# An FFT-mixing and gated feed-forward kernel on one core: batch 0 is turned on the TensorE instead of through DRAM

## The chip, the cores and the metric

The kernel runs on one core of a Trainium2 chip. The metric is the device time of one execution in microseconds (us). A number called "the time" is a median over several executions. Every kernel here was timed in alternation with the kernel before on the same chip. A program on one core has no second die to compare with, so an execution counts as fast unless it is over 1.5% above the fastest of its kernel.

Engines are named as in the profile: PE is the TensorE's matmuls, PEld its weight loads (loads of the stationary operand), DVE the VectorE, ACT the ScalarE, POOL the GpSimd, SP the SyncE, which issues DMAs here. "Granted clock" is the share of full speed that the TensorE's clock gate granted, so 0.50 is half speed.

## The reference

```python
def _attn_ref(x):                       # x: (8, 3008, 256) float32
    X = np.fft.fft(x, axis=1)
    X = np.fft.fft(X, axis=2)
    return X.real.astype(np.float32)

def _moe_ref(x, w_gate, w_val, w_out):  # x: the above as (24064, 256); weights 256x1536, 256x1536, 1536x256
    gate = np.maximum(x @ w_gate, 0.0)
    val = x @ w_val
    return (gate * val @ w_out).astype(np.float32)
```

## The kernel before

Each batch has 3008 = 94 x 32 rows. Row 32a + j of x lies on partition a, and a transform of 94 points over a is done for each of the 32 residues j (stage 1). Its result is `t1`, a tile of 96 partitions. A transform over the 32 residues follows (stage 2), and for it the residues must lie on partitions: `t4`, 128 partitions by 12 groups. The 256-point transform over the columns is folded into the weights (`fold_w`, three blocks of two matrices with a cosine and a sine part, on the PE), because x is folded about its middle column. From then on the kernel is a long pipeline of steps: two gate matmuls, value matmuls, elementwise products on ACT, DVE and POOL, and output matmuls. The first 12 steps have no output matmuls yet. They carry the rest of the weight folds instead.

For all batches but the first, x is loaded and folded ahead of time on POOL. Batch 0 has no such time, so its products use the unfolded rows: four matmuls for each row, with 96-column tables as the stationary operand and x as the moving one.

```python
def first_products(c, upper):                    # batch 0, stage 1; c = 0..7, two rows for each c
    if not upper:
        psf[c] = early("ps1")
    for i in range(2):
        jj = 2 * c + i
        o = psf[c][0:96, i * D:(i + 1) * D]
        v = xt[0]["hi"][...] if upper else xt[0]["lo"][0:NA, jj, :]
        back = free(v, D - 1, [-1, H - 1])       # the row read backwards
        ...                                      # (cut: which table is which)
        for k, (lo, hi, w, rhs) in enumerate(((0, H + 1, ce, v[:, 0:H + 1]), (1, H, ce, back),
                                              (H + 1, D, up, v[:, 1:H]), (H + 1, D, dn, back))):
            nc.tensor.matmul(o[:, lo:hi], lhsT=w, rhs=rhs, start=not (upper or i or k),
                             stop=upper and i == 1 and k == 3, skip_group_check=True)
```

The change of partitions goes through DRAM, for batch 0 as for the others, and one column then needs a rotation:

```python
def shuffle_out(b, c0, c1, q=nc.sync):
    q.dma_start(out=view(Td[b], 2 * c0 * D, [[16 * D, 96], [1, 2 * (c1 - c0) * D]]),
                      in_=t1t[b][:, 2 * c0:2 * c1, :].rearrange("p j d -> p (j d)"))

def shuffle_in(b, a0, a1):
    ...
    nc.sync.dma_start(out=t4t[b][:, a0:a1, :],
                      in_=view(Td[b], a0 * 128 * D, [[D, 128], [128 * D, a1 - a0], [1, D]]))

def rotate(b, a0=0, a1=NKA, evac=nc.scalar.copy):
    t4 = t4t[b]
    ps = borrow("psr") if b or a0 else early("psr")
    nc.tensor.matmul(ps[:, a0:a1], lhsT=rot[:], rhs=t4[:, a0:a1, H], start=True, stop=True)
    evac(t4[:, a0:a1, H], ps[:, a0:a1])
```

The start of the program, in the order in which it is issued, cut to its core:

```python
WARM = 16
def warm(n):                                     # dummy matmuls on zeros, 512 columns each
    for k in range(n):
        nc.tensor.matmul(psk[:], lhsT=wk[:, 512:640], rhs=wk[:, 0:512], start=True, stop=True)
warm(WARM)
...                                              # loads, tables; then, in three groups:
group((1, 2, 3), False); ...; group((1, 2, 3), True); ...; shuffle_out(0, 1, 4)
group((4, 5), False); group((4, 5), True); ...; shuffle_out(0, 4, 6)
group((6, 7, 0), False); group((6, 7, 0), True); ...
shuffle_out(0, 6, 8); shuffle_out(0, 0, 1, nc.scalar)
...
shuffle_in(0, 0, 4); shuffle_in(0, 4, NKA)
...
warm(10)
pair_w(0, 0, dve)                                # sums and differences of weight blocks
...
fold_w(0, 0, 0, "act"); fold_w(0, 0, 1, "dve"); fold_w(0, 1, 0, "act")   # during the shuffle
rotate(0, 0, 4, dve.tensor_copy)
stage2(0, 0, 0, "act"); stage2(0, 0, 1, "dve")
fold_w(0, 1, 1, "act")
```

`group(cs, upper)` calls `first_products(c, upper)` for each c.

The later batches' work is placed at numbered steps. For batch 1 the shuffle is at step 25 and its rotation at step 29, where PE meets the wait:

```python
    sh, tr, t2 = (22, 28, (29, 30, 32, 34, 35, 37)) if b else (25, 29, (30, 31, 33, 34, 35, 37))
    at(t0 + sh, shuffle_out, b + 1, 0, 8)
    at(t0 + sh, shuffle_in, b + 1, 0, NKA)
    at(t0 + tr, rotate, b + 1)
    for i, k in enumerate(t2):
        at(t0 + k, stage2, b + 1, i // 2, i % 2, "act")
```

## Time and profile before

| What | Value | View |
|---|---|---|
| time | 629.67 us (629.32 to 629.78, 3 runs) | timed runs |
| span of the profiled execution | 630.0 us (its device time was 632.18) | page |
| products of batch 0 on PE | 7.42 to 15.1 us | timeline of PE |
| DRAM shuffle of batch 0 | out 3.65 us, in 2.89 us | chain of waits |
| first gate matmul, first output matmul | 24.57 us, 55.70 us | timeline of PE |
| PE's wait on batch 1's shuffle | 2.05 us, up to 92.84 us | timeline of PE |
| PE busy from 200 to 600 us | 398.79 of 400 us | table by stretches |

Two lines of the page of the kernel before: the busy time of each engine with its share of the span and the number of instructions, and the granted clock in tenths for 40 equal slices (about 15.8 us each; 9 means 90% or more).

```profile
PE 614.4 (98%) x4288; PEld 411.3 (65%) x4320; DVE 537.9 (85%) x644; ACT 439.4 (70%) x842; POOL 513.4 (81%) x439
PEclk9899999999999999999999999999999999999999
```

PE is busy nearly always, so a change of the start is worth what it does to PE's start and no more. Next, the timeline of PE in the kernel before: start in us, duration in us, engine, line, operation, output and inputs, stationary rows x columns, moving rows x columns, count; in brackets an idle time before it and what released it.

```profile
7.42 0.33 PE L197 MATMUL ps<-lo,w 94*96 94x129 bf16 x3
7.59 0.22 PE L197 MATMUL ps<-lo,n 94*96 94x127 bf16 x1
7.64 0.33 PE L197 MATMUL ps<-lo,w 94*96 94x129 bf16 x3
...
22.42 0.17 PE L216 MATMUL psr<-t,rot 128*128 128x4 bf16 x1 [1.77 <-DMA t<-Td]
...
24.57 0.59 PE L555 MATMUL G<-pq,wc 128*128 128x496 bf16 x1
...
55.70 0.60 PE L619 MATMUL po<-wo,h 128*128 128x256 bf16 x4
```

Four product matmuls take 0.22 us (7.42 to 7.64): PE streams columns almost without a pause. After the last product PE does dummies and weight folds, and then waits 1.77 us for the shuffle. The chain of waits of the kernel before (start, length, what) has the shuffle in full:

```profile
15.76 3.65 DMA Td<-t
19.49 2.89 DMA t<-Td
```

The waits of PE in the kernel before (what waited, for what: us in total, times, longest):

```profile
PE psr L216 <- DMA t<-Td: 3.8, 2, 2.0
PE V L570 <- DVE h L583: 2.0, 3, 0.9
```

The first line holds both shuffles that PE waits for: 1.77 us for batch 0 and 2.05 us for batch 1. The table by stretches of the kernel before gives, after the stretch and its length in us, the busy us (instructions) of PE, PEld, DVE, ACT and POOL, the granted clock, the DMA share and GB/s:

```profile
6.00:12.00 6.00, 6.00 (x86) 5.15 (x84) 4.48 (x17) 3.88 (x10) 5.69 (x16) 1.00 1.07 188
12.00:18.00 6.00, 5.88 (x64) 4.17 (x65) 5.12 (x17) 3.19 (x9) 1.82 (x7) 1.00 0.86 303
18.00:24.00 6.00, 4.20 (x24) 1.57 (x20) 3.22 (x6) 1.75 (x3) 0.00 (x0) 0.98 0.56 172
24.00:30.00 6.00, 5.38 (x18) 1.75 (x16) 2.80 (x6) 3.39 (x6) 3.71 (x4) 0.74 1.10 393
```

After the idle time near 21 us the clock falls for about 3 us (0.74 on average from 24 to 30 us).

### The profile page before, as it was taken

How to read it: one execution, taken by the hardware profiler on the slowest of the kernel's cores; microseconds unless marked ns; L12 is line 12 of the kernel's file. 1: busy time of each engine (PE TensorE's matmuls, PEld its weight loads, DVE VectorE, ACT ScalarE, POOL GpSimd, SP SyncE). 2: the span in 40 equal slices, each digit the busy share in tenths (PEclk: the TensorE clock that was granted, in tenths of full speed). 3: DMA queues.
4: the chain of work that ended last, by engine and by line, in shares of the span. 5: the costliest groups of instructions: out<-in, count | busy, mean ns of one | idle time of the engine just before them, and what ended most of it. 6: DMA issues, size and time to landing. Idle time of an engine off the chain costs nothing.

```text
span 630.0 us, 11979 instructions
## 1 busy us (share of the span) xinstructions
PE 614.4 (98%) x4288; PEld 411.3 (65%) x4320; DVE 537.9 (85%) x644; ACT 439.4 (70%) x842; POOL 513.4 (81%) x439
## 2 busy tenths in 40 slices
PE   9899989999999999999999999999999999999996
PEld 6225656666666666666666666666666666666665
DVE  7677978998988998998988988899988989899991
ACT  5357768777777777777777777777687777766660
POOL 7358998998989998998989999899988866565664
PEclk9899999999999999999999999999999999999999
DMA  8878146613734254622725146432722123312113
GB/s 180 272 158 160 43 132 180 152 33 89 213 89 105 66 172 104 162 61 64 209 76 147 34 117 191 105 101 50 214 75 71 33 83 99 78 32 66 35 34 98
DMA packets 34737, 69.01 MB, mean 110 GB/s; under 512 B 5963, under 2 KB 23058, under 8 KB 31346
## 3 DMA queue, kind: packets, MB, share of 16 engines
q1 hardware_dynamic: 29974, 52.85, 31.5%
q0 software_dynamic: 4432, 15.11, 9.9%
q8 instruction: 33, 0.54, 0.4%
q10 hardware_dynamic: 272, 0.30, 0.2%
q14 instruction: 26, 0.21, 0.1%
HBM read 39.63 MB, written 30.96 MB: 112 GB/s over the span
## 4 chain that ended last, share of the span: by engine, by line
PE 93%; DMA 3%; POOL 1%; issue 1%; DVE 1%; ACT 0%; POOLq 0%; DVEq 0%; SPq 0%
PE po L619 39%; PE V L570 19%; PE G L555 10%; PE G L562 10%; PE G L556 9%; PE ps L159 2%; PE ps L228 2%; PE psw L285 1%; DMA Td<-t 1%; DMA t<-Td 1%; DMA lo<-in_x_dram 1%; DVE h L583 1%; PE ps L197 0%; POOL hi L129 0%; PE ps L163 0%
## 5 line engine op out<-in xcount | busy, mean ns | idle before, releaser
L590 POOL TENSOR_TENSOR h<-gm,E 128x992 bf16<-128x992 f32 (+1 forms) x138 | 319.7, 2317 | 79.1 <-DVE E L597 49.6
L619 PE MATMUL po<-wo,h 128*128 128x256 bf16 (+2 forms) x2304 | 328.5, 272 | 0.5
L619 PEld LDWEIGHTS <-h 128*128 128x128 bf16 (+2 forms) x2304 | 231.4, 103 | 105.9
L564 ACT ACTIVATE gm<-G 128x496 f32<-128x496 f32 (+1 forms) x288 | 170.4, 592 | 94.5 <-PE G L562 85.0
L583 DVE TENSOR_TENSOR h<-gs,V 128x1024 bf16<-128x1024 f32 (+3 forms) x150 | 173.8, 1159 | 63.1 <-PE V L570 43.2
L577 DVE SCALAR_TENSOR_TENSOR E<-nb,af,V 128x496 f32<-128x496 bf16 (+1 forms) x276 | 190.1, 730 | 0.0
L557 ACT ACTIVATE gs<-G 128x497 f32<-128x497 f32 (+2 forms) x288 | 169.6, 589 | 25.4 <-PE G L556 25.4
L597 DVE SCALAR_TENSOR_TENSOR E<-E,V 128x992 f32<-128x992 f32 (+1 forms) x138 | 164.4, 1191 | 0.0
L555 PE MATMUL G<-pq,wc 128*128 128x497 bf16 (+2 forms) x288 | 108.4, 376 | 1.2
L562 PE MATMUL G<-pq,wm 128*128 128x496 bf16 (+1 forms) x288 | 108.1, 375 | 0.1
L556 PE MATMUL G<-pq,ws 128*128 128x497 bf16 (+2 forms) x288 | 108.2, 376 | 0.0
L570 PE MATMUL V<-pq,ws 128*128 128x512 bf16 (+2 forms) x279 | 83.7, 375 | 0.0
L570 PE MATMUL V<-pq,wc 128*128 128x496 bf16 (+2 forms) x266 | 80.9, 375 | 0.0
L556 PEld LDWEIGHTS <-ws 128*128 128x128 bf16 x288 | 28.2, 98 | 32.8 <-issue 0.3
L632 ACT COPY os<-po 128x512 f32<-128x512 f32 x63 | 36.9, 585 | 14.7 <-PE po L619 13.0
L570 PEld LDWEIGHTS <-wc 128*128 128x128 bf16 x288 | 28.2, 98 | 21.9 <-issue 3.8
L110 POOL TENSOR_TENSOR eo<-xla 94x254 bf16<-94x254 f32 x56 | 40.1, 727 | 1.1
L555 PEld LDWEIGHTS <-wc 128*128 128x128 bf16 x288 | 28.2, 98 | 19.1 <-issue 1.9
L174 ACT CAST t<-ps 96x512 bf16<-96x512 f32 x60 | 35.0, 583 | 5.6 <-PE ps L197 3.2
L107 POOL TENSOR_TENSOR xla<-xla,xha 94x510 f32<-94x510 f32 x28 | 35.4, 1264 | 2.2
L110 POOL TENSOR_TENSOR eo<-xlb 94x254 bf16<-94x254 f32 (+1 forms) x42 | 34.2, 814 | 0.8
L562 PEld LDWEIGHTS <-wm 128*128 128x128 bf16 x288 | 28.2, 98 | 7.0 <-issue 3.5
(119 smaller groups left out, 360.1 us busy)
## 6 DMA issues: line engine op xcount, KB each, us to landing
out_dram<-os SPq DMA_DIRECT2D x124, 128.0 KB
Td<-t SPq DMA_DIRECT2D x7, 768.0 KB
t<-Td SPq DMA_DIRECT2D x7, 768.0 KB
out_dram<-os SPq DMA_DIRECT2D x82, 64.0 KB
xla<-in_x_dram SPq DMA_DIRECT2D x7, 720.0 KB
xlb<-in_x_dram SPq DMA_DIRECT2D x7, 640.0 KB
nb<-Nd SPq DMA_DIRECT2D x23, 128.0 KB
out_dram<-os SPq DMA_DIRECT2D x40, 48.0 KB
```

The costliest lines, as they stand in the source:

```text
L110: yield eng.tensor_tensor(e1[:, :, o:o + H - 1], x1[:, :, 1:H], free(x1, D - 1, [D, n], [-1, H - 1]), op=op)
L555: nc.tensor.matmul(G[:, ds], lhsT=wc[0][:, fs], rhs=pq[:, 0, ds], start=True, stop=False)
L556: nc.tensor.matmul(G[:, ds], lhsT=ws[0][:, fs], rhs=pq[:, 1, ds], start=False, stop=True)
L557: nc.scalar.activation(pair(t, "gs")[:, t % 2, ds], G[:, ds], ACTF.Relu)
L562: nc.tensor.matmul(G[:, cols], lhsT=wm[0][:, f * 128:(f + 1) * 128], rhs=pqt[b, blk][:, 1, cols], start=False, stop=True, skip_group_check ...
L564: nc.scalar.activation(pair(t, "gm")[:, t % 2, cols], G[:, cols], ACTF.Relu)
L570: nc.tensor.matmul(pair(t, "V")[:, t % 2, cs], lhsT=w[:, f * 128:(f + 1) * 128], rhs=pqt[b, blk][:, min(k, 1), cs], start=(k == 0), stop=( ...
L577: nc.vector.scalar_tensor_tensor(pair(t, "E")[:, t % 2, cols], nbt[b, blk][:, cols], af[:, f:f + 1], pair(t, "V")[:, t % 2, cols], op0=ALU ...
L583: nc.vector.tensor_tensor(pair(t, "h")[:, k, 0, 0:ds.stop - ds.start], pair(t, "gs")[:, k, ds], pair(t, "V")[:, k, ds], op=ALU.mult)
L590: eng.tensor_tensor(free(pair(t, "h")[:], 1024 * (t % 2) + 512 + w - 1, [1024, n], [-1, w]), pair(t, "gm")[:, k, cols], val[:, k, cols], o ...
L597: nc.vector.scalar_tensor_tensor(E[:, :, cols], E[:, :, cols], 2.0, V[:, :, cols], op0=ALU.mult, op1=ALU.subtract)
L619: nc.tensor.matmul(po[0:m, i, :], lhsT=pair(t - f + ff, "h")[:, ff % 2, sg, g * 128:g * 128 + m], rhs=wo[:, ff, :], start=(ff == 0), stop= ...
```

## The change

The intent is to get rid of batch 0's way through DRAM. Stage 1 of batch 0 exchanges its operands: a row of x (128 columns of it) becomes the stationary operand and the tables (192 columns, both halves side by side) the moving one. The result then has the columns of x on its partitions, and matmuls with a permutation matrix ("uprights") can turn it so that the residues lie on partitions for stage 2. The permutation also does what the rotation did.

The half rows that the kernel before read backwards as moving operand become stationary ones, and for them reversed copies (`back`) are made on DVE and ACT beforehand. Column 0 of x has no mirror partner. It is added to lane 0 of the second half by a matmul of its own, whose stationary operand has one column. So each of the 32 rows now has two matmuls with 128 stationary columns and one with one column. The diff, cut to its core:

```diff
-WARM = 16
+WARM = 11
+FIRST = 15
...
+    def first_products(c, upper, k):
+
+        if not (upper or k):
+            psf[c] = early("ps1")
         for i in range(2):
             jj = 2 * c + i
-            o = psf[c][0:96, i * D:(i + 1) * D]
...
-            for k, (lo, hi, w, rhs) in enumerate(((0, H + 1, ce, v[:, 0:H + 1]), (1, H, ce, back),
-                                                  (H + 1, D, up, v[:, 1:H]), (H + 1, D, dn, back))):
-                nc.tensor.matmul(o[:, lo:hi], lhsT=w, rhs=rhs, start=not (upper or i or k),
-                                 stop=upper and i == 1 and k == 3, skip_group_check=True)
+            o = psf[c][:, 192 * i:192 * i + 192]
+            v = xt[0]["hi" if upper else "lo"][0:NA, r % 16, :]
...
+            if k:
+                nc.tensor.matmul(o, lhsT=tabs["back"][:, r, :], rhs=up, start=False, stop=upper and i == 1,
+                                 skip_group_check=True)
+                continue
+            nc.tensor.matmul(o, lhsT=v[:, H:D], rhs=dn, start=not (upper or i), stop=False, skip_group_check=True)
+            nc.tensor.matmul(o[0:1, 96:192], lhsT=v[:, 0:1], rhs=dc, start=False, stop=False, skip_group_check=True)
...
+    def upright(blk, cs, evac):
...
+        for g in range(4):
+            nc.tensor.matmul(ps[:, g * H:(g + 1) * H], lhsT=free(t1t[0][:], 1536 * cs + 128 * (4 * blk + g), [1, 128]),
+                             rhs=perm[:], start=True, stop=True)
...
         def group(cs, upper):
-            for c in cs:
-                first_products(c, upper)
+            for k in range(2):
+                for c in cs:
+                    first_products(c, upper, k)
...
-        shuffle_in(0, 0, 4)
-        shuffle_in(0, 4, NKA)
...
-        warm(10)
...
-        rotate(0, 0, 4, dve.tensor_copy)
+        fold_w(0, 0, 0, g_tile())
+        upright(0, 0, "act")
+        upright(0, 1, "dve")
+        fold_w(0, 0, 1, g_tile())
         stage2(0, 0, 0, "act")
         stage2(0, 0, 1, "dve")
...
-        sh, tr, t2 = (22, 28, (29, 30, 32, 34, 35, 37)) if b else (25, 29, (30, 31, 33, 34, 35, 37))
+        sh, tr, t2 = (22, 28, (29, 30, 32, 34, 35, 37)) if b else (25, 30, (31, 32, 33, 34, 35, 37))
```

Also cut: most sums and differences of weight blocks move from DVE to POOL, one fold moves behind the first gate, four uprights go into steps 1 to 6, batch 1's stage 1 and its rotation are re-spaced, and POOL's folding of the later batches' x and the order of some loads are rearranged.

## The prediction

> **What bounds the kernel.** The busy table gives PE 98% of the 630.0 us span; from 200 to 600 us PE is busy 398.8 of 400. The change leaves that alone. What it can move is the start: in the chain of waits the first gate matmul comes at 24.6 us, the first output matmul about 55 us.
>
> **The start in the trace.** The x loads keep the DMA engines near full to 12.2 us. Products follow to 15.1, then eviction 0.59, DRAM shuffle out 3.65, in 2.89, rotation, two stage-2 evictions, gate at 24.57. PE fills the hole with dummies and weight folds, yet idles from 20.65 to 22.42; the granted clock (table by stretches) then reads 0.50 from 24 to 27 us, about 1.7 us lost. The Trainium skill ("TensorE: Matmul & The Clock Gate", Part 1) describes such half-clock windows of about 3.4 us after an idle one; here a gap of 1.8 us was enough. From 24.6 to 55.0 the twelve steps take 30.4 us; PE is busy 27.6 of them; it waits 2.0 us for DVE h, behind weight pairings on DVE (one took 2.33 us, the others 0.69). At 90.2 PE waits 2.0 us for batch 1's shuffle.
>
> **Removed:** batch 0's shuffle (6.54 us on the chain), its rotation, fifteen dummy matmuls, most pairings on DVE.
>
> **Added:**
> - 32 reversals split between DVE and ACT: ten ops, together about 2 us on each (estimate from 0.58 us for 512 elements on ACT, 0.36 to 0.7 on DVE).
> - Products: 96 matmuls again, no change.
> - Six uprights (4 matmuls, about 0.24 us, and an eviction of 0.58 on ACT or 0.69 on DVE each); two lie before the gate.
> - Pairing moves to POOL, 1.27 us an op, six more ops: 7.6 us. POOL was idle from 14.2 to 26 and 33 to 40, so it fits, narrowly.
> - Longer last products: the reversals of rows 12 to 19 must follow the last loads, and the c=0 product waits in PSUM order for the c=4 eviction, which queues on ACT behind those reversals and two sines. I expect PE to idle about 2 us near 13 to 15 us, products done at about 17.5 instead of 15.1, perhaps a half-clock window after.
>
> **Sum.** Last products 17.5 (+2.4), eviction 0.9, fold 1.1 interleaved, uprights with eviction 1.2, stage 2 with eviction 1.3, gate near 22 (21.5 to 23.8): 1 to 3 us gained. One fold (1.05 us) moves behind the gate and takes part back; a half-clock window avoided is worth up to 1.7. Steps 0 to 11: stalls on DVE h mostly gone, 1 us of PE added: 1 to 2 us gained. Batch 1's rotation comes a step (2 us) later, its stage 1 ends earlier: its 2.0 us wait goes. Total about 5 us.
>
> **Prediction: 624.8 us, 80% range 621.3 to 628.6.** Faster by over 2%: 3%; within 2%: 96%; slower by over 2%: 1%.
>
> **Right if:** no shuffle DMA before 60 us; gate at 21.5 to 23.8; first output matmul at 50 to 53 us; no wait on batch 1's shuffle over 0.5 us; 200 to 600 us unchanged within 0.5 us.
>
> **Wrong if:** PE idle while ACT and DVE do reversals costs half-clock through stage 1 and the folds; weight pairs on POOL arrive late and steps 0 to 6 stall; delayed folds on POOL push batch 1's stage 1, restoring or enlarging the wait at 90 us. A larger gain, if no half-clock window falls.

## More of the kernel before

A sine fold ends with a scaled copy, `wm`, which reads the copy just made and not PSUM:

```python
    plain(ws[i][:, sl_], ps[:])
    nc.vector.tensor_scalar(wm[i][:, sl_], ws[i][:, sl_], scalar1=s2[:], scalar2=None, op0=ALU.mult)
```

## The result, and the profile after

The kernel after takes 636.88 us (636.09 to 637.15, 4 runs) against 629.72 us (629.32 to 630.85, 4 runs) of the kernel before in the same rounds. The ratio is 1.0109, with a 95% interval of 1.0091 to 1.0126. Ratios here are the mean time of one kernel's fast runs over that of the other's of the same rounds, so they are not quite the ratio of the medians quoted. The change costs about 1%. The prediction had a gain of 0.8%, and the result lies outside its range.

The same two lines of the page, for the kernel after:

```profile
PE 623.3 (98%) x4264; PEld 412.4 (65%) x4295; DVE 539.7 (85%) x647; ACT 442.2 (70%) x847; POOL 509.9 (80%) x446
PEclk7599999999999999999999999999999999999999
```

PE is still 98% busy, but it is busy 9 us longer, and the clock is 0.7 and then 0.5 in the first two slices. The timeline of PE in the kernel after, with the columns as above:

```profile
6.46 0.24 PE L215 MATMUL ps<-wn,lo 94*128 94x192 bf16 x1 [0.84 <-DVE wn L429]
6.63 0.26 PE L216 MATMUL ps<-wn,lo 94*1 94x96 bf16 x1
6.83 0.26 PE L215 MATMUL ps<-wn,lo 94*128 94x192 bf16 x1
...
10.00 0.34 PE L215 MATMUL ps<-wn,hi 94*128 94x192 bf16 x1
10.27 0.26 PE L216 MATMUL ps<-wn,hi 94*1 94x96 bf16 x1
10.46 0.34 PE L215 MATMUL ps<-wn,hi 94*128 94x192 bf16 x1
...
31.63 0.38 PE L602 MATMUL G<-pq,wc 128*128 128x496 bf16 x1
...
62.48 0.60 PE L666 MATMUL po<-wo,h 128*128 128x256 bf16 x4
```

The distance from one matmul to the next is what counts here, not the durations, which overlap. A pair of a 128-column and a one-column matmul takes 0.37 us at full clock (6.46 to 6.83; 0.38 over several pairs) and 0.46 us at half clock (10.00 to 10.46). The products end at 26.3 us, so they take 19.8 us instead of 7.7. The weight loads of the kernel after show why a pair is slow. In this timeline of PEld a line without a bracket had no idle time that the profile puts down to anything:

```profile
8.82 0.77 PEld L212 LDWEIGHTS <-back 94*128 94x128 bf16 x6
10.00 0.10 PEld L215 LDWEIGHTS <-hi 94*128 94x128 bf16 x1 [0.41 <-DMA hi<-in_x_dram,ixf]
10.27 0.08 PEld L216 LDWEIGHTS <-hi 94*1 94x1 bf16 x1 [0.17 <-issue]
```

The one-column load starts at 10.27 us, the very time at which its matmul is recorded, and 0.17 us after the load before it had ended. The PE loads, streams, and only then loads again. At full clock the sum agrees: the two loads take 0.10 and 0.08 us, and a pair that needn't wait for its loads takes 0.183 us (the run fullcol, below), in all 0.37 of the 0.38 us measured. In the run of six `back` loads at 8.82 us there is no such gap. The table by stretches of the kernel after:

```profile
6.00:12.00 6.00, 5.50 (x27) 2.63 (x27) 4.29 (x23) 2.98 (x8) 5.59 (x13) 0.69 1.05 179
12.00:18.00 6.00, 6.00 (x30) 2.98 (x29) 4.51 (x11) 2.82 (x8) 5.39 (x13) 0.50 0.56 181
18.00:24.00 6.00, 6.00 (x31) 3.03 (x30) 2.32 (x6) 0.82 (x2) 1.20 (x1) 0.50 0.37 111
```

From 12 to 24 us PE is counted busy all the time, yet the clock is at half, and only 30 matmuls (of 192 or 96 moving columns) go through in 6 us where the kernel before had 64 to 86 (most of about 128). PE's busy time does not show this. The Trainium skill warns of it ("Perfetto Trace Analysis", Identifying the Most-Contended Engine): matmul busy time is a poor measure of how near the PE is to its peak, and the busy share of the weight loads is a better one. This trace agrees: the loads' busy time falls from 5.15 and 4.17 of 6 us before to 2.98 after. Last, the waits of PE in the kernel after:

```profile
PE psk L390 <- DVE wk L384: 1.3, 1, 1.3
PE V L617 <- DVE h L630: 1.1, 2, 0.6
```

The waits on a shuffle are gone. The two profiled spans (630.0 and 635.2 us) therefore add up like this: gate 7.06 us later; first output matmul 6.78 us later; batch 1's wait of 2.05 us gone; PE idle for 0.50 us more from 100 to 200 us (99.29 busy us against 99.79); in sum 6.78 - 2.05 + 0.50 = 5.2 us. From 200 to 600 us PE is busy 398.79 us in both. The profiled execution of the kernel before was a slower one of its kind (632.18 us), which is why the spans differ by less than the medians.

### The profile page after: what moved, and what is told of

It is laid out like the page before. It is cut to its first block, busy times and chain, and to the rows that moved or that the text cites. A ratio compares the mean times of both kernels' runs of the same rounds, so it can differ in the third digit from the quotient of the medians.

```text
span 635.2 us, 11938 instructions
## 1 busy us (share of the span) xinstructions
PE 623.3 (98%) x4264; PEld 412.4 (65%) x4295; DVE 539.7 (85%) x647; ACT 442.2 (70%) x847; POOL 509.9 (80%) x446
## 4 chain that ended last, share of the span: by engine, by line
PE 94%; DVE 2%; DMA 1%; issue 1%; SPq 1%; ACT 0%; POOL 0%; POOLq 0%; DVEq 0%
PE po L666 39%; PE V L617 18%; PE G L602 10%; PE G L609 9%; PE G L603 9%; PE psw L324 2%; PE ps L163 2%; PE ps L266 2%; PE ps L215 1%; PE ps L216 1%; PE ps L212 1%; DMA t<-Td 1%; DMA Td<-t 1%; SPq L717 1%; DVE h L630 0%
## 5 line engine op out<-in xcount | busy, mean ns | idle before, releaser
L114 POOL TENSOR_TENSOR eo<-xla 94x256 bf16<-94x256 f32 (+1 forms) x56 | 35.1, 638 | 0.8
L178 ACT CAST t<-ps 96x512 bf16<-96x512 f32 x56 | 32.7, 584 | 2.4 <-PE ps L163 0.2
L114 POOL TENSOR_TENSOR eo<-xlb 94x256 bf16<-94x256 f32 (+3 forms) x42 | 29.9, 712 | 0.9
```

The source lines that it names most:

```text
L114: yield eng.tensor_tensor(e1[:, :, k * (H + 1):k * (H + 1) + H - k], free(x1, H - k, [D, n], [-1, H - k]), x1[:, :, H + k:D], op=op)
```

## The experiments

Twelve kernels were run. The rival theories for the 12 us that the products lost were:

- A: matmuls with 128 and with one stationary column in turn keep the PE from loading weights ahead, and the sparse stream that follows drops the clock.
- B: the clock falls because of too few dummies or of idle gaps, and the products are slow only because of the clock.
- C: the tables as moving operand, read with a stride, stream slowly.

The first four runs were timed together. In their rounds the kernel before took 631.70 us, 1.5 to 1.9 us more than in the later rounds: four of its seven runs there had a mean clock of 0.994 to 0.996. So "as fast as before" is a mild test in these four.

### no_onecol: the one-column matmuls taken away (wrong result)

```diff
-            nc.tensor.matmul(o[0:1, 96:192], lhsT=v[:, 0:1], rhs=dc, start=False, stop=False, skip_group_check=True)
```

> The 32 one-column matmuls of the products are left out (the result is wrong on purpose: one term of one row is missing). Theory A (changing between a 128-column and a 1-column weight stops weight loads from running ahead, which doubles the product stage and starves the clock gate): the product matmuls start about 0.08 us apart at full clock, the last ends at 15 to 17.5 us, first gate at 21 to 24 us, total 623 to 628 us. Theory B (the shortened warm-up and the gaps while loads arrive let the clock drop, whatever the matmuls are): the clock still reads 0.50 from about 8 us on and the products last beyond 20 us, total above 632 us.

630.19 us against 631.70 of before; ratio 0.9994 (0.9963 to 1.0024). The result was wrong as planned (relative error 0.033). The gate comes at 23.81 us instead of 31.63. So nearly all of the loss goes with 32 small matmuls, although the clock still falls to 0.50 from 10.4 to 20.7 us. A low clock by itself is not the main cost. Two parts of A's expectation missed: the products end at 18.6 us (15 to 17.5 expected), and the total lies above its range. This kernel removes the matmul, its strided moving operand and the change of width together, so it can't tell A from C; the next run does.

### fullcol: the same matmuls with 128 stationary columns (wrong result)

```diff
-            nc.tensor.matmul(o[0:1, 96:192], lhsT=v[:, 0:1], rhs=dc, start=False, stop=False, skip_group_check=True)
+            nc.tensor.matmul(o[:, 96:192], lhsT=v[:, 0:H], rhs=dc, start=False, stop=False, skip_group_check=True)
```

> The one-column matmuls stay, with the same moving operand and its stride, but take 128 columns as weights instead of 1 (wrong on purpose). Theory A: as good as leaving them out plus 32 x 0.04 us, so 624 to 629 us, pairs about 0.13 us apart at full clock. Theory C (the moving operand that hops 1535 elements is what is slow): the pairs stay 0.38 us apart at full clock and 0.47 at half, total 635 us or more. Theory B: 635 us or more.

629.85 us against 631.70; ratio 0.9975 (0.9934 to 1.0015). The relative error is 0.26, as the edit adds columns that don't belong there. The number of matmuls and the moving operand are as in the kernel after; only the loads are larger. The timeline of PE in fullcol:

```profile
6.54 0.26 PE L216 MATMUL ps<-wn,lo 94*128 94x96 bf16 x1
6.64 0.25 PE L215 MATMUL ps<-wn,lo 94*128 94x192 bf16 x1
6.73 0.26 PE L216 MATMUL ps<-wn,lo 94*128 94x96 bf16 x1
```

A pair now takes 0.19 us here (6.54 to 6.73; 0.183 over more of them) instead of 0.38, though it loads 256 columns instead of 129. The larger load is the faster one because all widths are equal. C falls, and so does the idea that the one-column load is itself slow. (With the stationary width the edit also widens the output from one partition to 128; these two can't be parted.) The clock was at 0.50 from 9.6 to 23.2 us here too, after idle gaps of 0.28 and 0.61 us, and still the time was that of before: the order of the widths is the larger share of the loss. The total is just above A's range (624 to 629).

### warm16: the five dummies put back

```diff
-WARM = 11
+WARM = 16
```

> Only the warm-up goes back from 11 to 16 dummy matmuls. Theory A: PE is dense to about 7.6 us instead of 5.6, but the product stage stays sparse and drops the clock all the same: 635 to 638 us, clock 0.50 for at least 12 us in the product stage. Theory B: clock stays at 1.0 for most of the products, total 624 to 630 us.

637.48 us against 631.70; ratio 1.0107 (1.0071 to 1.0142), the same as the kernel after. The clock fell at 11.0 us instead of 8.3 and stayed at 0.50 until 28. The first output matmul came at 63.44 us. A longer warm-up delays the fall and saves nothing: B in its first form falls. Before the clock fell, PE was idle for only 0.15 us (6.31 to 6.46 us) from the first dummy on.

### grouped: the same matmuls, the one-column ones in a pass of their own

```diff
-            if k:
+            if k == 2:
                 nc.tensor.matmul(o, lhsT=tabs["back"][:, r, :], rhs=up, start=False, ...)
                 continue
+            if k == 1:
+                nc.tensor.matmul(o[0:1, 96:192], lhsT=v[:, 0:1], rhs=dc, start=False, ...)
+                continue
             nc.tensor.matmul(o, lhsT=v[:, H:D], rhs=dn, start=not (upper or i), stop=False, ...)
-            nc.tensor.matmul(o[0:1, 96:192], lhsT=v[:, 0:1], rhs=dc, start=False, ...)
...
-            for k in range(2):
+            for k in range(3):
```

> Correct result: within each group all 128-column products come first, then all one-column ones, then the reversed ones, so the width of the weights changes three times a group instead of at every matmul. Theory A, as a matter of changes of width: one-column matmuls run about 0.05 to 0.08 us apart, products end at 16 to 19 us, total 624 to 630 us. Theory A', that a one-column matmul is slow whatever stands before it: they stay 0.15 to 0.2 us apart, total 630 to 635 us. Theory B: no change, 636 to 638 us.

630.34 us against 631.70; ratio 0.9983 (0.9951 to 1.0015), with a right result. Nothing was taken away; only the order of the same matmuls differs from the kernel after. The timeline of PE in grouped:

```profile
6.01 0.66 PE L218 MATMUL ps<-wn,lo 94*128 94x192 bf16 x6
6.59 0.78 PE L216 MATMUL ps<-wn,lo 94*1 94x96 bf16 x6
```

Six one-column matmuls take 0.78 us with the latency of the last one, about 0.10 us from one to the next (A expected 0.05 to 0.08 and a total of at most 630 us, A' 0.15 to 0.2). That is what the same matmul costs with 128 stationary columns in fullcol (0.183 less 0.084 us), so one column isn't slow among its like. The products end at 19.3 us, the gate is at 25.01 and the first output matmul at 56.38. The clock still reads 0.50 from 15.9 to 22.7 us, so grouping cures the order and leaves a second fault, the gaps in PE's work.

### before_onecol: the one-column matmuls added to the kernel before, on zeros

```diff
                 nc.tensor.matmul(o[:, lo:hi], lhsT=w, rhs=rhs, start=not (upper or i or k), ...)
+                if k == 0:
+                    nc.tensor.matmul(o[0:1, 0:96], lhsT=v[:, 0:1], rhs=wk[0:NA, 0:96], start=False, stop=False,
+                                     skip_group_check=True)
```

> The kernel before, plus the suspected cost alone: 32 one-column matmuls put between its 96-column product matmuls, with the same x column as weights and zeros as moving data (adds nothing, the result stays correct). Theory A (changes of weight width serialise and starve the clock): each costs about 0.25 us at full clock, so the product stage grows by 8 us or more, the clock falls to 0.50 within it, and the total rises by 6 to 14 us to 636 to 644 us. Rival (the products were slow in the changed kernel for another reason, such as weights taken from x): rise of at most 32 x 0.04 = 1.3 us.

636.06 us against 630.18; ratio 1.0089 (1.0071 to 1.0108), and the result is right, as `wk` holds zeros. So the loss can be put into the kernel before by this alone. The timeline of PE:

```profile
7.52 0.22 PE L197 MATMUL ps<-lo,w 94*96 94x129 bf16 x1
7.67 0.20 PE L200 MATMUL ps<-wk,lo 94*1 94x96 bf16 x1
7.81 0.31 PE L197 MATMUL ps<-lo,w 94*96 94x127 bf16 x2
...
8.01 0.22 PE L197 MATMUL ps<-lo,w 94*96 94x129 bf16 x1
```

A row takes 0.49 us (7.52 to 8.01) where before it took 0.22, and the products last from 7.52 to 23.3 us, 8.1 us longer than before. Half of the expectation missed: the clock did not fall (0.998 on average). As an estimate from the 0.22 us of a 512-column matmul at full clock, the five matmuls of a row stream 606 columns in 0.26 us, so PE streams about half of the time here, and about a third of it in the kernel after (288 columns, 0.12 of 0.38 us). Half was enough to keep the clock up here; that share alone doesn't decide, for in fullcol a pair streams about two thirds of its time (0.12 of 0.183 us), and after two gaps the clock fell all the same.

### before_tr30: batch 1's rotation a step later, in the kernel before

```diff
-        sh, tr, t2 = (...) if b else (25, 29, (30, 31, 33, 34, 35, 37))
+        sh, tr, t2 = (...) if b else (25, 30, (31, 32, 33, 34, 35, 37))
```

> The kernel before with one part of the change alone: batch 1's rotation at step 30 instead of 29, its first two stage-2 pieces one step later. My reading that PE waited 2.0 us there for the shuffle and that one step (about 2 us) hides it: wait under 0.5 us, total 1.5 to 2.1 us lower, about 0.9970 of before. Rival (the shuffle ends later still or PE only waits elsewhere): within 0.3 us of before.

628.32 us against 630.18 in five rounds; ratio 0.9965 (0.9949 to 0.9980). PE's wait on batch 1's shuffle is gone. This small part of the change is worth having alone, and needs nothing else of it. In the profiled execution part of it went into another wait: PE waited 1.6 us for DVE's E.

### dense: grouped, and nine dummies in the gaps

```diff
+                    if not (upper or k):
+                        warm({0: 4, 5: 1}.get(c, 0))
                     first_products(c, upper, k)
+            if 1 in cs:
+                warm(1 if upper else 3)
```

> The grouped order plus nine dummy matmuls of 512 columns where PE idled in the product stage (three and one after the first group, one before c=5, four before c=0). Theory D (what is left of the loss is the half clock from 16 to 22.6 us, which the idle PE caused): clock stays 1.0, last product at 17 to 18 us instead of 19.3, first gate at 21.5 to 22.5 instead of 25.0, total 2.5 to 3.5 us below grouped, 0.993 to 0.996 of before. Rival (the one-column matmuls count as idle for the gate and it falls all the same): no more than 0.7 us below grouped.

629.03 us against 630.18; ratio 0.9969 (0.9954 to 0.9985). The table by stretches of dense, to be set beside the same stretch of the kernel after:

```profile
12.00:18.00 6.00, 6.00 (x56) 4.11 (x55) 5.61 (x12) 2.26 (x6) 5.12 (x12) 1.00 0.68 219
```

The clock is 1.00 throughout, and the gate comes at 22.74 us, inside the range predicted for the whole change (21.5 to 23.8). The sizes that theory D named for this run were missed: the last product ends at 18.5 us (17 to 18 expected), the gate is 0.24 us late, and the ratio is not in 0.993 to 0.996. The first output matmul is at 55.43, later than predicted: 32.69 us lie between the two, where the kernel before has 31.13 and before_tr30 has 29.58. Part of that is one instruction. The timeline of DVE in dense:

```profile
40.12 2.33 DVE L333 TENSOR_SCALAR wm<-ws,s 128x512 bf16<-128x512 bf16 x1 [0.73 <-ACT ws L328]
```

The scaled copy takes 0.35 us when POOL is quiet and 2.33 here, beside POOL's work, and an upright behind it waits 1.05 us. The Trainium skill ("GPSIMD Engine Reference", Specifications) says that POOL shares its SBUF interfaces with the VectorE, with contention for DVE's two-port modes or two SBUF inputs. The next two kernels test it.

### dense_plus: one scaled copy reads PSUM, and the c = 0 product has a PSUM buffer of its own

```diff
-            psf[c] = early("ps1")
+            psf[c] = early("ps1") if c else psg.tile([128, 512], F32, tag="g", name="ps1")
...
-        nc.vector.tensor_scalar(wm[i][:, sl_], ws[i][:, sl_], scalar1=s2[:], ...)
+        nc.vector.tensor_scalar(wm[i][:, sl_], wps[n, i, 1][:] if (n, i) == (0, 1) else ws[i][:, sl_], scalar1=s2[:], ...)
...
-                        warm({0: 4, 5: 1}.get(c, 0))
+                        warm({0: 2, 5: 1, 6: 2}.get(c, 0))
```

> Dense, plus a PSUM buffer of its own for the c=0 product (no wait for the c=4 eviction, so only two dummies before it and two before c=6), plus the second scaled weight copied from PSUM instead of SBUF. In the grouped run this 0.35 us copy took 1.44 us while POOL was pairing weights, and PE then waited 1.05 us. If that is contention for the SBUF port shared by DVE and POOL, the copy from PSUM takes 0.7 to 0.8 us whatever POOL does, PE's wait falls to under 0.5 us, and the total is a further 0.5 to 1.5 us below dense. If not, the copy still takes over 1.2 us.

629.01 us against 630.18; ratio 0.9979 (0.9958 to 1.0001), and the gate at 22.75 us. The gate didn't move, and the first output matmul came 0.5 us earlier (54.93). The one copy from PSUM took 0.75 us, as expected, but of those left in SBUF three took about 0.35 us and two took 1.83 and 1.07. The expected gain of 0.5 to 1.5 us didn't come: the time can't be told apart from dense.

### dense_psum: five of six scaled copies read PSUM

```diff
-        nc.vector.tensor_scalar(wm[i][:, sl_], wps[n, i, 1][:] if (n, i) == (0, 1) else ws[i][:, sl_], scalar1=s2[:], ...)
+        nc.vector.tensor_scalar(wm[i][:, sl_], ws[i][:, sl_] if (n, i) == (0, 0) else wps[n, i, 1][:], scalar1=s2[:], ...)
```

> Dense_plus, with five of the six scaled weight copies read from PSUM instead of SBUF. In the dense run one of these copies from SBUF, 0.35 us alone, took 2.33 us beside POOL and made PE wait 1.05 us at 42 us. If the SBUF port shared with POOL is the cause: every one of the five takes 0.65 to 0.8 us, no wait of PE over 0.7 us in steps 0 to 11, total 0.5 to 1.5 us below dense_plus, about 0.995 of before. If the copies are slow for another reason, they stay spread from 0.35 to over 1 us and the total stays.

627.76 us against 629.84 in five rounds (627.26 to 632.38; the one high run had a mean clock of 0.990, the others 0.998 or 0.999); ratio 0.9974 (0.9946 to 1.0003). The same copy in the timeline of DVE in dense_psum:

```profile
40.28 0.75 DVE L335 TENSOR_SCALAR wm<-psw,s 128x512 bf16<-128x512 f32 x1 [0.73 <-ACT ws L328]
```

From PSUM each of the five copies takes 0.75 us, in place of 0.35 to 2.33. POOL runs the same instructions beside it in both kernels, 0.57 us later in dense_psum. The skill's page "VectorE: DVE Perf Modes" (Why PSUM operands drop a tier) says that a PSUM operand keeps DVE from the two-port mode; the trace agrees in both ways, slower than the best case and not disturbed. The first output matmul comes at 53.89 us, 1.5 us before dense's. In the time this doesn't show beyond the noise: the ratios of dense, dense_plus and dense_psum (0.9969, 0.9979, 0.9974) lie within each other's intervals.

### dense_psum_tr29: the same, with batch 1's rotation back at step 29

```diff
-        sh, tr, t2 = (...) if b else (25, 30, (31, 32, 33, 34, 35, 37))
+        sh, tr, t2 = (...) if b else (25, 29, (30, 31, 33, 34, 35, 37))
```

> The same, with batch 1's rotation put back to step 29, so that what is left against before is the start without DRAM shuffle alone, in its best form here. If my reading is right that the start is worth only about 1 us against before: total about 1.7 to 2 us above dense_psum, 0.3 to 1.3 us below before (0.998 to 0.9995). If the start is worth what I predicted (3 us or more), it is 0.995 or less of before.

629.45 us against 629.84; ratio 0.9994 (0.9975 to 1.0013). A wait of PE in dense_psum_tr29:

```profile
PE psr L256 <- DMA t<-Td: 1.6, 1, 1.6
```

The wait on batch 1 is back, and the gain is gone: five of the six runs of dense_psum lie below all six of this kernel. So a start without the DRAM shuffle, even mended, is worth nothing that five rounds can show; the interval leaves room for at most 1.6 us. What remains of the change's gain is the rotation's step.

### before_tr30_psum: the two mends that need no new start, together

```diff
-            nc.vector.tensor_scalar(wm[i][:, sl_], ws[i][:, sl_], scalar1=s2[:], scalar2=None, op0=ALU.mult)
+            nc.vector.tensor_scalar(wm[i][:, sl_], ps[:], scalar1=s2[:], scalar2=None, op0=ALU.mult)
```

on top of before_tr30.

> The kernel before with the later rotation and its six scaled copies read from PSUM. In its trace these copies took 0.35 to 0.69 us, so little is to be gained: within 0.5 us of before_tr30, about 0.9965 of before. If dense_psum is not below this one by more than 0.7 us, removing the DRAM shuffle is worth nothing here even when its one-column matmuls and its clock are mended.

629.49 us against 629.84; ratio 0.9993 (0.9974 to 1.0012). This missed: it was expected to be as good as before_tr30. The copies took 0.75 us from PSUM as elsewhere, but the PSUM buffer is now held until DVE has read it, and PE waited 1.35 us for that (the wait of `psw` on DVE's `wm`). The first output matmul comes at 54.62 us, against 53.18 in before_tr30. The mend that helped one schedule in its trace costs the other. By the test set beforehand dense_psum would have passed, as its median is 1.7 us below this one; but this control was spoiled by its own new wait, so the test decides nothing. What remains is the comparison with before_tr30, from other rounds.

### filled: the kernel after with dense's nine dummies, still in alternation

```diff
+                    if not (upper or k):
+                        warm({0: 4, 5: 1}.get(c, 0))
                     first_products(c, upper, k)
+            if 1 in cs:
+                warm(1 if upper else 3)
```

> The changed kernel with the nine dummy matmuls of the dense run at the same places, but with the one-column matmuls still alternating with the 128-column ones. It parts the two halves of the loss: serialised matmuls and half clock. If the alternating pairs themselves stream too little (192 + 96 columns in 0.38 us, about a third of the time) to hold the clock, the clock falls to 0.50 in the product stage all the same and the total is 636 to 639 us. If only the idle gaps dropped it, the clock stays 1.0, pairs stay 0.38 us apart, the last product ends at about 22 to 23 us instead of 26.3, and the total is 632 to 634 us.

641.26 us against 630.22 (636.44 to 641.45, 4 runs); ratio 1.0147 (1.0103 to 1.0192). The table by stretches of filled, the same stretch as for dense:

```profile
12.00:18.00 6.00, 6.00 (x29) 2.85 (x29) 2.59 (x11) 2.96 (x8) 5.03 (x12) 0.50 0.54 170
```

The gaps are filled as in dense, PE is counted busy 6.00 of 6 us in both, and the clock is 0.50 here and 1.00 there. The stretch before, in which the clock falls, first in filled and then in dense:

```profile
6.00:12.00 6.00, 5.54 (x26) 2.68 (x26) 4.30 (x23) 2.98 (x8) 5.59 (x13) 0.70 1.05 189
6.00:12.00 6.00, 5.37 (x46) 3.58 (x48) 5.26 (x27) 4.07 (x12) 5.59 (x13) 1.00 1.02 178
```

The clock falls at 8.3 us in filled, before the first of the nine dummies (9.75 us), so the dummies could only have brought it back, and they didn't. Up to there PE had idled less in filled (0.82 us before the first product) than in dense (1.23 us), and in warm16 it had idled 0.15 us. So the alternation itself is what brings the clock down and holds it there, at this sparseness (before_onecol alternates too and kept its clock); gaps are not needed for it. B falls in its second form too. The total is above the expected 636 to 639 us: the dummies run at half clock as well. Three of the four runs were at 641 us with a mean clock of 0.978 to 0.980. The one at 636.44 had 0.990, so the clock was probably at half for a shorter time in it (only one execution is profiled).

## Why the prediction was wrong

**Right.** No shuffle DMA is issued before 60 us; the first is at 90.84. The wait on batch 1's shuffle is gone, as predicted for a later step (2.05 us; alone 0.9965). From 200 to 600 us nothing changed. The time of the gate, predicted at 21.5 to 23.8 us, is what the mended kernels reach (22.74 to 22.86), so the arithmetic of the chain from load to gate was sound but for the products (in dense they end at 18.5 us instead of 17.5, and the rest of the chain takes 4.2 us instead of 4.5). Stalls on DVE h went from 2.0 to 1.1 us.

**The step that failed: "Products: 96 matmuls again, no change."** The number was wrong for the kernel before (128), and that mattered little. The size was wrong for the kernel after: the products took 19.8 us and not 7.7. 32 of the 96 matmuls have one stationary column and stand between ones with 128. At the change of width the next load does not run ahead of the matmul in flight, so load and stream add up. The Trainium skill ("TensorE: Matmul & The Clock Gate", Architectural detail) says that the PE's queue can pull weight loads ahead; before's trace shows that for equal widths. Estimated from the distances measured at full clock (0.38 us for each of 32 pairs, 0.084 us for each of 32 `back` matmuls), the products would take 14.9 us, and 8.5 us with the distance of fullcol (0.183): 6.3 us are the alternation. The other 4.9 us of the 19.8 are the half clock, which the sparse stream itself brings on. The fold and uprights behind it lost another 1.2 us to it (1.91 against 1.01 us, 0.80 against 0.55). Shown by runs: the order alone carries the loss (grouped against after, before_onecol against before), the width and not the count (fullcol), the clock follows from the alternation (filled against dense). That 6.3 and 4.9 us are the exact shares is an estimate.

The prediction did fear the half clock, but for another reason: PE idle while ACT and DVE reverse rows. Such gaps do cost clock (grouped, 15.9 to 22.7 us), and nine dummies cure them (dense). The larger fall came while PE was counted busy.

**"Steps 0 to 11: 1 to 2 us gained."** This term failed too. The stalls were half gone, but the moved fold (1.0 us) and four uprights (0.9 us) put 1.8 us of PE work into these steps (29.17 busy us in dense_psum, 27.36 in before_tr30), and the copies beside POOL grew. From gate to first output matmul the kernel after takes 30.85 us, before 31.13 with a half-clock window in it, before_tr30 29.58 without one.

**"A half-clock window avoided is worth up to 1.7."** The window is in the profiled execution of before, which took 632.18 us with a mean clock of 0.996. Of the 36 timed runs of before in the experiments' rounds, 22 have a clock of 0.998 or 0.999, with a median of 629.8 us, and 12 have 0.994 to 0.996, with a median of 631.7; the two ranges overlap (629.0 to 631.8 and 630.0 to 632.4). So in most rounds the window is absent from the median, and could not be gained there.

**Where the shuffle's 6.54 us went.** Even where the products are mended, the start is worth nothing (dense_psum_tr29, 0.9994). The hole in PE's work before the rotation, 15.1 to 22.4 us, held 3.45 us of weight folds that must be done anyway, 2.1 us of dummies and 1.8 us of idle time. Only the last two, 3.9 us, could be gained. One fold and the uprights, later products (18.5 us against 15.1) and the copies took it back.

**Which version is best.** before_tr30 (0.9965) and dense (0.9969) beat the kernel before by more than the noise. dense_psum (0.9974) has the lowest median, 627.76 us, but its interval reaches 1.0003. These runs can't tell the three apart, and all are faster than the kernel after. before_tr30 is a change of one line.

**Open.** Why a change of width stops the loads from running ahead is not visible in a trace, and neither is what exactly drops the clock. With PE counted busy throughout, it fell while PE streamed about a third of the time (after) and held at about a half (before_onecol); once at half clock, the same pairs stream about half of the time (estimated 0.24 of 0.46 us), and it stayed down. After gaps it fell at higher shares too (fullcol), so no threshold follows from these runs.

## What to carry to other kernels

Cost a small matmul by what it does to its neighbours' weight loads, not by its columns: keep matmuls of one stationary width together, and look at the distance from matmul to matmul, because a PE counted as busy can be at half clock and stream a third to a half of the time. Before removing a wait from the start, subtract the useful work that already fills it; and take the value of a half-clock window from several timed runs with their clocks, not from one profiled execution.

## What the Trainium skill lacked or had wrong

- "TensorE: Matmul & The Clock Gate", Architectural detail and the weight-load section: it tells that loads run ahead, and names row groups or the background weight buffer as a condition, but not that stationary operands of 128 and one columns in turn don't. Measured 0.38 us a pair against 0.183 us with equal widths.
- The same page, LDWEIGHTS (loading the stationary operand): its time in ns, columns over 1.2, gives 107 for 128 columns, 94 for 113, 80 for 96 and under 1 for one column. The trace of the kernel after has 98, 131, 124 and 79 ns, so the formula is near for the first alone.
- The same page, Part 1: it ties the half clock to an idle window of about 3.4 us (and speaks further on of frequent short idle times in one kernel). Here a gap of 1.77 us was enough in one execution of before, one of 0.90 us in grouped, while 1.23 us (dense) and 1.29 us (before_tr30) were not; and a PE counted busy 6.00 of 6 us was held at 0.50 for 20 us by alternating widths (kernel after, filled).
- "GPSIMD Engine Reference", Specifications: this page names the contention with the VectorE without a size (other pages of the skill say more of the shared port). A 128x512 bf16 copy on DVE went from 0.35 us to as much as 2.33 us in dense and 2.38 us in warm16; from PSUM it was 0.75 us in dense_psum.
